# Strassen steps of an MLP behind linear attention on Trainium2: which engine makes the low parts, and when the weight sets are made

## The chip, the cores and the metric

The kernel runs on one core of a Trainium2 chip. [...] An engine works through its queue in order; semaphores make it wait for others. The metric is the time of one execution in microseconds, lower is better.

## What is computed

Linear attention over 8 batches and 8 heads, with a feature map of exponentials, and behind it an MLP on its output, all in float32. Cut to what matters:

```python
def phi(x):
    proj = np.einsum('bhsd,df->bhsf', x, w_phi)
    proj = proj - np.max(np.abs(proj), axis=-1, keepdims=True)
    return np.concatenate([np.exp(proj), np.exp(-proj)], axis=-1)
q_p, k_p = (phi(q), phi(k))
kv = np.einsum('bhsf,bhsd->bhfd', k_p, v)
z = np.sum(k_p, axis=2)
num = np.einsum('bhsf,bhfd->bhsd', q_p, kv)
den = np.einsum('bhsf,bhf->bhs', q_p, z)[..., None] + 1e-06
# x: num / den, as 4608 tokens of 512 features
h = x @ w_in          # 512 x 2048
g = h - np.tanh(h)
return (g @ w_out).astype(np.float32)   # 2048 x 512
```

## The kernel before

**The attention** runs over 32 units of one batch and two heads. `ramp` starts the first three, `period(i)` runs for units 3 to 31 and `drain` ends them. A period takes five units at different stages: it projects unit i, sums the keys of unit i-1 (`kadd`, four operations on POOL), multiplies unit i-2 (`num`), computes the denominator of unit i-3, and divides and stores unit i-5 (`den_mul` on POOL, `x_store` on SP's queue). The denominator goes through DRAM: `den_recip_load` loads it as tile dn, DVE takes the reciprocal (L409), `den_store` writes rr, and in the next period `den_spread` reads it back as rb on all partitions; `den_mul` waits for rb. These DMAs, `x_store` and the loads of v all stand in SP's queue.

In each period DVE also decodes one tile of the weights, which arrive as 64-bit floats: 16 of w_in ("i") and 16 of w_out ("o"), 128x512 each.

**The second stage** multiplies x by w_in with Strassen's seven products instead of eight. Tokens go in 6 groups of 768, features in 8 sets k of two tiles: 48 steps q = 8g + k, called frames. Each product is six matmuls of 384 columns, as both operands are split into a high part in a rounded format and a low part, the remainder (high x high, high x low, low x high). `Prep` makes a set's seven weight operands, high and low: four sums (`sums`, `sums2`), four casts on ACT (`hi`), four subtractions on POOL (`lo`). Sets 0 and 1 are made in the attention (`aside_at`), sets 2 to 7 in frames 0 to 5, two frames ahead. A finished set lies in one of three ring slots; frames 0 to 7 store it to DRAM (`ring_store`, one DMA of 1792 KB), later frames load it two ahead (`ring_load`).

A frame issues, in this order on PE: products p1 and p2, a chunk, p6, a chunk, p5 and p7, a chunk, p4 and p3, a chunk. The products accumulate in two PSUM banks, A and B, that have one buffer each. ACT copies A after p1, p6 and p5 (`part`, L748) and at the end (L762); DVE adds B to these copies: `add11` (L752) after p2, `add22` (L755) after p7, `add21` (L759) after p4. So p4 waits for `add22`, and the next p2 for `add21`. The adds give h as two tiles of 128x768, x (its diagonal quarters) and y (the others). g = h - tanh(h) is then a chain for each: squares, tanh and a mask on ACT (`a_sq`, `a_th`, `a_mk`), five operations on DVE (`v_1`, `v_23` which is two, `v_4`, `v_5`), and the split into a cast on ACT (`a_gh`, L796) and the low part gl on POOL (L797). The chain of y runs in the next frame, between that frame's own adds. A chunk multiplies half of such a tile by w_out, 9 matmuls of 512 columns, six chunks behind its products (`LAG`).

`hooks` places the rest: for group g+1 four operand sums (`x_sum`) and seven operand splits (`x_op`: cast on ACT, low part `x_low`), mostly on POOL, in frames 6 and 7 and the next frame 0; six evictions of finished results (`evict`) in frame 1; in group 0 also `Prep` and `wo_split`, the high and low parts of w_out (the first four are made in the attention). All queues are in the order in which the Python code is written (manual schedule).

Of the kernel before, what the change touches and what calls it, by code (L numbers as in the profile page):

```python
# [33 lines left out]
def tile_linear_attention_moe(  # L34
# [21 lines left out]
    EARLY_O = 4  # L56
    EARLY_K = 2
# [8 lines left out]
    XO_FIRST = (0, 1, 6)  # L66
    assert PC % HT == 0 and NCT == 4 and DM == 4 * P
# [32 lines left out]

    class Prep:
        def __init__(self, k, tags):
            self.k, self.tags = k, tags

        def steps(self):
            w0, w1 = (wi[2 * self.k + n] for n in range(2))
            a, b = slice(0, 2 * P), slice(2 * P, 4 * P)
            sub = nc.gpsimd.tensor_tensor

            def sums():  # L110
                self.r = ring_tile(self.k)
                self.s = [st_any(t, [P, 2 * HT], f"s{self.k}_{t}")[:, 0:DM].rearrange("p (n f) -> p n f", n=2) for t in self.tags]
                s = self.s
                sub(s[0][:, 1], w1[:, a], w1[:, b], ALU.add)
                sub(s[1][:, 0], w0[:, a], w1[:, a], ALU.subtract)

            def sums2():
                s = self.s
                sub(s[0][:, 0], s[0][:, 1], w0[:, a], ALU.subtract)
                sub(s[1][:, 1], w0[:, b], s[0][:, 0], ALU.subtract)  # L120

            def hi(n, m, src):
                nc.scalar.copy(self.r[:, 0, n:m], src())

            def lo(n, m, src):
                sub(self.r[:, 1, n:m], src(), f32(self.r[:, 0, n:m]), ALU.subtract)
# [4 lines left out]
            return [
                (None, sums),
                (None, sums2),
# [973 lines left out]
```

## Time and profile before

| what | us |
|---|---|
| runs before | 1175.53 median of 3 (1172.7 to 1176.58) |
| profiled execution | 1174.16, its span 1172.4 |
| PE busy | 1096.5 (94% of the span) |
| DVE busy | 1005.7 (86%) |
| ACT busy | 847.3 (72%) |
| POOL busy | 636.9 (54%) |

The profile is of one execution. "Busy" adds up the times in which an engine worked, so an average hides stages that have different limits; the prediction therefore reads it by stage. Rows of the timeline give start and duration in us, engine, line, operation, what was written and read, and in brackets the idle time ahead of it with what ended it. Rows of groups give total busy us and the mean in ns. Rows of waits give who waited for whom: us in total, times, longest.

### The profile page before, as it was taken

The page shows a single profiled execution, that of the slowest core. Times are in us where ns is not written, and L with a number is a line of the kernel's source. Part 1 is how long each engine was busy: PE and PEld are TensorE (multiplying, and loading weights), DVE is VectorE, ACT ScalarE, POOL GpSimd, SP SyncE. Part 2 cuts the span into 40 slices and gives each one's busy share as a digit, 9 for nine tenths or more (in the row PEclk, how much of TensorE's full clock was granted, in tenths as well). Part 3 has the DMA queues.
Part 4 walks back from the last instruction along what each step waited for, and adds up shares of the span by engine and source line. Part 5 has one row for each costly group of instructions (what it writes and reads, how often), then busy time and mean ns, then how long its engine had stood idle before and what let it go on. Part 6 is the DMA issues. An engine that isn't in the chain of part 4 may idle for free.

```text
span 1172.4 us, 19032 instructions
## 1 busy us (share of the span) xinstructions
PE 1096.5 (94%) x7244; PEld 909.2 (78%) x7244; DVE 1005.7 (86%) x1062; ACT 847.3 (72%) x1321; POOL 636.9 (54%) x397
## 2 busy tenths in 40 slices
PE   8999999999878788899989999999998999889998
PEld 6666666676567677788878898878987889778986
DVE  7999988999878788988889878988789888898777
ACT  5787887777766566777767776777767777677775
POOL 4788787877598986622464225532356224632222
PEclk9999999999979888999999999999999999999999
DMA  5677778766624124245313541344232443234301
GB/s 179 189 230 218 220 222 250 217 210 192 212 112 180 63 87 165 70 184 200 136 63 145 185 153 66 126 166 148 109 126 73 170 180 126 78 142 149 126 1 55
DMA packets 57676, 173.57 MB, mean 148 GB/s; under 512 B 13680, under 2 KB 28400, under 8 KB 51440
## 3 DMA queue, kind: packets, MB, share of 16 engines
q1 hardware_dynamic: 43184, 139.97, 34.0%
q10 hardware_dynamic: 14400, 32.38, 9.2%
q8 instruction: 57, 0.93, 0.3%
q14 instruction: 35, 0.29, 0.1%
HBM read 138.48 MB, written 33.70 MB: 147 GB/s over the span
## 4 chain that ended last, share of the span: by engine, by line
PE 54%; DVE 27%; ACT 8%; issue 4%; POOL 3%; DMA 2%; POOLq 0%; DVEq 0%; SPq 0%; ACTq 0%
PE A L708 9%; PE B L708 7%; PE pc L322 6%; PE po L819 5%; PE po L820 5%; PE po L825 5%; DVE thy L788 5%; PE po L371 5%; DVE s2y L785 4%; DVE s2y L784 3%; PE pu L385 3%; DVE s2y L791 3%; PE pj L256 2%; DVE s1x L781 2%; PE pa L256 2%
## 5 line engine op out<-in xcount | busy, mean ns | idle before, releaser
L797 POOL TENSOR_TENSOR glx<-s2x,ghx 128x768 fp32r<-128x768 f32 x48 | 103.1, 2149 | 290.8 <-ACT ghx L796 282.7
L708 PE MATMUL A<-xo,wr 128*128 128x384 f32 x1152 | 245.5, 350 | 5.3 <-ACT u L748 4.0
L708 PE MATMUL B<-xo,wr 128*128 128x384 f32 x864 | 185.5, 350 | 53.1 <-DVE hx L755 45.7
L708 PEld LDWEIGHTS A<-xo,wr 128*128 128x128 f32 x1152 | 215.6, 196 | 20.1 <-ACT u L748 5.0
L708 PEld LDWEIGHTS B<-xo,wr 128*128 128x128 f32 x864 | 157.1, 195 | 68.4 <-DVE hx L755 57.9
L797 POOL TENSOR_TENSOR gly<-s2y,ghy 128x768 fp32r<-128x768 f32 x47 | 92.2, 1962 | 133.3 <-ACT ghy L796 119.6
L748 ACT COPY u<-A 128x384 f32<-128x384 f32 x144 | 69.2, 481 | 101.4 <-PE A L708 100.8
L781 DVE SCALAR_TENSOR_TENSOR s1x<-s1x,yx 128x768 f32<-128x768 f32 x48 | 62.4, 1300 | 80.7 <-ACT s1x L770 80.2
L796 ACT CAST ghy<-s2y 128x768 fp32r<-128x768 f32 x47 | 39.2, 835 | 108.2 <-DVE s2y L791 108.2
L819 PE MATMUL po<-who,ghx 128*128 128x512 f32 x288 | 117.4, 407 | 0.0
L820 PE MATMUL po<-wlo,ghx 128*128 128x512 f32 x288 | 116.0, 403 | 0.0
L820 PE MATMUL po<-wlo,ghy 128*128 128x512 f32 x288 | 113.4, 394 | 0.0
L819 PE MATMUL po<-who,ghy 128*128 128x512 f32 x288 | 113.3, 393 | 0.0
L785 DVE SCALAR_TENSOR_TENSOR s2y<-s2y,hy 128x768 f32<-128x768 f32 x48 | 106.5, 2218 | 1.7
L311 ACT ACTIVATE kp<-t 64x256 f32<-64x256 f32 (+1 forms) x126 | 88.4, 726 | 2.1 <-DVE t L275 1.0
L825 PE MATMUL po<-who,glx 128*128 128x512 f32 x288 | 83.0, 396 | 6.9 <-POOL glx L797 6.9
L788 DVE TENSOR_TENSOR thy<-hy,thy 128x768 f32<-128x768 f32 x47 | 74.4, 1583 | 10.1 <-ACT thy L775 10.1
L825 PE MATMUL po<-who,gly 128*128 128x512 f32 x282 | 80.2, 392 | 0.0
L322 PE MATMUL pc<-kp,v 128*64 128x256 f32 x640 | 76.1, 384 | 0.0
L422 POOL TENSOR_TENSOR d<-d,rb 128x576 f32<-128x576 f32 x32 | 46.8, 1462 | 50.3 <-DMA rb<-rr 31.7
L791 DVE COPY_PREDICATED s2y<-yy,thy 128x768 f32<-128x768 uint32 x47 | 67.6, 1439 | 5.6 <-ACT u L748 0.5
L825 PEld LDWEIGHTS po<-who,glx 128*128 128x128 f32 x288 | 53.7, 188 | 21.6 <-POOL glx L797 9.5
(184 smaller groups left out, 2640.3 us busy)
## 6 DMA issues: line engine op xcount, KB each, us to landing
wr<-wd SPq DMA_DIRECT2D x40, 1792.0 KB, 7.3
qk<-in_qkT ACTq DMA_DIRECT2D x27, 576.0 KB, 6.0
wd<-wr SPq DMA_DIRECT2D x8, 1792.0 KB, 5.6
v<-in_v SPq DMA_DIRECT2D x32, 320.0 KB, 4.4
rb<-rr SPq DMA_DIRECT2D x64, 144.0 KB, 4.4
xs<-d SPq DMA_DIRECT2D x32, 288.0 KB, 5.7
out<-o SPq DMA_DIRECT2D x35, 256.0 KB, 2.0
rawo<-in_moe_w_out ACTq DMA_DIRECT2D x16, 512.0 KB, 4.4
```

Of the source, the lines that this page charges most:

```text
L311: nc.scalar.activation(u.kp[h, :, j, s, :], u.t[r][h, :, x, :], AF.Exp, scale=1.0 - 2.0 * s)
L322: nc.tensor.matmul(u.pc[e * D : (e + 1) * D, 0 : 2 * F], u.v[:, j, e, :], u.kp[:, e, j, :, :], start=(j == first), stop=(j == last))
L708: nc.tensor.matmul(bank[:, 0:HT], w[:, a, n, cs], x[:, b, c, :], start=start and i == 0, stop=i == 5, skip_group_check=not start,)
L748: nc.scalar.copy(t, A[q][:, 0:HT])
L781: nc.vector.scalar_tensor_tensor(z.s1, z.s1, PC1, z.y, ALU.add, ALU.mult)
L785: nc.vector.scalar_tensor_tensor(z.s2, z.s2, PA, z.h, ALU.mult, ALU.mult)
L788: nc.vector.tensor_tensor(z.th, z.h, z.th, ALU.subtract)
L791: nc.vector.copy_predicated(z.s2, z.y.bitcast(U32), z.th)
L797: nc.gpsimd.tensor_tensor(z.gl, z.s2, f32(z.gh), ALU.subtract)
L819: nc.tensor.matmul(po, z.gh[:, ts], wh, start=first, stop=False)
L820: nc.tensor.matmul(po, z.gh[:, ts], wl, start=False, stop=False)
L825: nc.tensor.matmul(po, z.gl[:, ts], wh, start=False, stop=last)
```

## The change

1. **POOL's work of the second stage goes to DVE**: gl (`v_gl`), the operand sums and low parts, the low parts of w_out (but three in the head). DVE's order gets `v_gl(xp)` between `v_2` and `v_3`, and `v_gl(yp)` behind `add22`. The high parts of w_out all go to ACT, and five of six evictions too. The operand work of the next group spreads over frames 4 to 7 and the next frame 0.
2. **Seven weight sets are made in the attention** (2 to 6, then 0 and 1), on POOL and ACT, and stored from there in pieces; the order in which weight tiles are decoded follows. Set 7 is made by DVE in frames 2 to 4. Low parts of w_out are no longer made in the attention.
3. **The ring is in pieces**: three tiles a set (products 0 and 1; 2 and 3; 4 to 6), two slots instead of three, each loaded when its products of two frames before are done.
4. **The first two steps are interleaved**: `drain` makes the operands of group 0 and the first two products between the last attention steps, and `head` runs steps 0 and 1 together on two pairs of PSUM banks, with the chain of x of step 0 in two halves.

```diff
-    EARLY_O = 4
-    EARLY_K = 2
+    EARLY_K = 7
+    EARLY_O = 3
+    XS = 10
...
-    wd = [dram.tile([P, 14 * 2 * P], F32, name=f"wd{k}") for k in range(NFP)]
+    PARTS = ((0, 2), (2, 4), (4, 7))
+    wd = [[dram.tile([P, 2 * (b - a) * 2 * P], F32, name=f"wd{k}_{a}") for a, b in PARTS] for k in range(NFP)]
...
+    order = [*range(2, EARLY_K), 0, 1, *range(EARLY_K, NFP)]
+    outs = [("o", f) for f in range(NF)]
+    tiles = []
+    for n, k in enumerate(order):
+        tiles += [("i", 2 * k), ("i", 2 * k + 1), outs[n]]
+    tiles += outs[NFP:]
...
+    def ring_store(q, n, a=0, b=None, queue=nc.sync):
+        queue.dma_start(wd[q % NFP][n][:, a:b], flat(ring[q][n])[:, a:b])
...
+        aside = collections.defaultdict(lambda: ([], [], []))
+        for n, k in enumerate(order[:EARLY_K]):
+            p = Prep(k, nc.gpsimd, early_tile, early_stage).steps()
+            o = 5 + 7 * (n // 2) + 3 * (n % 2)
+            acts = ((1, "h2"), (2, "h4 h6"), (3, "h0")) if n % 2 == 0 else ((2, "h2 h6"), (3, "h4 h0"))
+            work = (
+                ((0, "s1 s3 s2"), (1, "s4 l2"), (2, "l4 l6"), (3, "l0"))
+                if n % 2 == 0
+                else ((0, "s1"), (1, "s3 s2 s4"), (2, "l2 l6"), (3, "l4 l0"))
+            )
+            for which, x in enumerate((acts, work)):
+                for d, names in x:
+                    aside[o + d][which].extend(p[nm] for nm in names.split())
+            if True:
+                when = (3, 4, 5, 5) if n % 2 else (2, 3, 4, 5)
+                for d, (part, a, b) in zip(when, ((1, 0, 1024), (2, 0, 768), (2, 768, 1536), (0, 0, 1024))):
+                    aside[o + d][2].append(lambda k=k, part=part, a=a, b=b: ring_store(k, part, a, b))
+        aside[30][1].extend(lambda n=n: x0_sum(n) for n in range(2))
+        aside[31][1].append(lambda: x0_sum(2))
+
+        def aside_at(i, late):
+            for f in aside[i][0] if not late else aside[i][1] + aside[i][2]:
+                f()
...
-            act, low = aside_at(i)
-            if act:
-                act()
+            if i < NU - 1:
+                aside_at(i, False)
...
             kadd(c)
-            if low:
-                low()
+            aside_at(i, True)
...
+            x0_sum(3, nc.vector)
+            x0_split(1)
...
+            w = dec[NU - 2]
+            dec_0(w, ps_t.tile([P, 2, 512], F32, tag="pt", name="pt"))
+            num_copy(p)
+            dec.append(dec_load(NU - 1, nc.scalar))
             pu = bank()
+            denom(p, pu)
+            dec_1(w)
+            dec_2(w)
+            dec_3(w)
+            ops(2)
+            num(c)
+            lows[2]()
+            den_mul(r)
             ksum(c, pu)
-            denom(p, pu)
...
+            product(A[0], 0, 0, 0, True)
...
+            product(Bk[0], 0, 1, 1, True)
...
-            num(c)
-            w = dec[NU - 1]
-            dec_0(w, ps_t.tile([P, 2, 512], F32, tag="pt", name="pt"))
+            ops(3)
             num_copy(c)
+            ops(6, 5, 4)
             dec_1(w)
             dec_2(w)
             dec_3(w)
+            for m in (3, 6, 5, 4):
+                lows[m]()
             denom(c, bank())
             denom_copy(c)
...
-            nc.scalar.copy(z.gh, z.s2)
-            nc.gpsimd.tensor_tensor(z.gl, z.s2, f32(z.gh), ALU.subtract)
...
+            nc.scalar.copy(z.gh[:, s], z.s2[:, s])
+
+        def v_gl(z, s=ALL):
+            nc.vector.tensor_tensor(z.gl[:, s], z.s2[:, s], f32(z.gh[:, s]), ALU.subtract)
...
-            nc.gpsimd.tensor_tensor(o, a, b, ALU.subtract)
...
+            nc.vector.tensor_tensor(o, a, b, ALU.subtract)
+
+        def ring_load(q, n):
+            nc.sync.dma_start(flat(ring_tile(q, n)), wd[q % NFP][n])
...
+        def head():
+            X0, X1 = slice(0, HT), slice(HT, 2 * HT)
+            ring_load(2, 0)
+            part(0, "u1")
+            add11(0)
+            ps_o.tile([P, 512], F32, tag="o", name="o")
+            p1p2(1, ps_o, "oo")
...
+            p6(0)
+            part(1, "u1")
+            add11(1)
...
+            part(0, "u2")
+            a_th(x, X0)
+            v_1(x, X0)
+            v_2(x, X0)
...
+            p5(0)
+            p7(0)
+            part(1, "u2")
+            part(0, "u4")
+            ring_load(2, 1)
+            a_gh(x, X0)
+            p5(1)
...
+            add22(0)
+            v_gl(x, X0)
+            a_sq(x, X1)
...
+            splits = [wo_split(f, nc.gpsimd if f < EARLY_O else nc.vector) for f in range(4)]
+            for f in (0, 1):
+                for step in splits[f]:
+                    step()
...
+            p4(0)
+            p3(0)
+            ring_load(2, 2)
+            add21(0)
+            a_mk(x, X1)
+            v_3(x, X1)
...
+            p7(1)
+            add22(1)
+            v_gl(x, X1)
+            v_1(y)
+            chunk(6)
+            p4(1)
+            add21(1)
+            v_2(y)
+            p3(1)
...
+            chunk(7)
+            v_5(y)
+            for f in (2, 3):
+                splits[f][0]()
+            a_sq(X[1])
+            a_gh(y)
+            for f in (2, 3):
+                splits[f][1]()
...
+        def late_head():
+            x, y = X[1], Y[0]
+            a_th(x)
+            v_1(x)
+            v_gl(y)
+            a_mk(x)
+            v_2(x)
+            v_3(x)
+            v_4(x)
...
+            if q == 2:
+                late_head()
+            else:
                 a_sq(yp)
-            if xp:
                 v_5(xp)
                 a_gh(xp)
...
+            if q == 2:
+                a_sq(yp)
+                v_5(xp)
+                a_gh(xp)
...
-            if yp:
-                v_1(yp)
-                a_th(yp)
-                v_23(yp)
+            v_1(yp)
+            a_th(yp)
+            v_2(yp)
+            v_gl(xp)
+            v_3(yp)
...
-            if yp:
-                a_gh(yp)
+            if q == 2:
+                v_4(yp)
+                v_5(yp)
+            a_gh(yp)
             at("a6")
+            v_gl(yp)
...
-            p4p3(q)
+            p4(q)
+            p3(q)
...
+            if q + 2 < NQ:
+                for n, at in enumerate(("a2", "a5", "end")):
+                    h[at].append(lambda n=n: ring_load(q + 2, n))
+            if g and k == 0:
+                op("a4", g, 6, "a6")
+            if g and k == 1:
+                for t, at in enumerate(("a2", "a2", "a3", "a5", "a5", "a6")):
+                    h[at].append(lambda t=t: evict(g - 1, t, nc.vector if t == 1 else nc.scalar))
+            if nxt < NG:
+                if k == (2 if g else 4):
+                    h["end" if g else "a2"].append(lambda: x_loads(nxt))
+                if 4 <= k < 7:
+                    for n in ((0, 1), (2,), (3,))[k - 4]:
+                        h["a3" if g else "end"].append(lambda n=n: x_sum(nxt, n))
+                    op("a4" if g else "end", nxt, k - 4, "a6" if g else "end")
+                if k == 7:
+                    op("a2", nxt, 3, "a3")
+                    op("a4", nxt, 4, "a6")
+                    op("end", nxt, 5, "end")
             if g == 0:
-                h["start"].append(lambda: ring_store(q))
...
-                op("a2", g, 4, nc.gpsimd, "a2")
-                op("a4", g, 5, nc.gpsimd, "a4")
-                op("a5", g, 6, nc.vector, "a6")
-            if g and k == 1:
-                h["a2"].append(lambda: evict(g - 1, 0, nc.scalar))
-                h["a2"].append(lambda: evict(g - 1, 1, nc.vector))
-                h["a3"].append(lambda: evict(g - 1, 2, nc.scalar))
-                h["a5"].append(lambda: evict(g - 1, 4, nc.scalar))
-                h["a6"].append(lambda: evict(g - 1, 3, nc.vector))
-                h["a6"].append(lambda: evict(g - 1, 5, nc.vector))
...
-                if k == 6:
-                    for n, at in enumerate(("start", "a2", "a4")):
-                        h[at].append(lambda n=n: x_sum(nxt, n))
-                    op("a4", nxt, 0, nc.gpsimd, "a6")
-                if k == 7:
-                    op("a2", nxt, 1, nc.gpsimd, "a2")
-                    op("a4", nxt, 2, nc.gpsimd, "a4")
-                    op("a5", nxt, 3, nc.vector, "a6")
-                    h["a4"].append(lambda: x_sum(nxt, 3))
-            if g == 0:
-                if k + 2 < NFP:
-                    steps = Prep(k + 2, (3, 4)).steps()
-                    for (act, pool), at in zip(steps, ("start", "start", "a2", "a4", "a6", "end")):
-                        if act:
-                            h[at].append(act)
-                        h[at].append(pool)
-                for n, at in ((0, "a6"), (1, "end")):
-                    f = EARLY_O + 2 * k + n
...
+                for p in PREP.values():
+                    for kk, at, names in (
+(2, "end", "s1 s3 s2 s4"),
+                        (3, "a3", "h2 l2 h4"),
+                        (3, "end", "l4 h6"),
+                        (4, "a3", "l6"),
+                        (4, "end", "h0 l0"),
...
+                for n, at in enumerate(("a6", "a7")):
+                    f = 2 * k + n
+
+                    def hi(f=f):
+                        split[f] = wo_split(f, nc.vector)
+                        split[f][0]()
+
+                    h["a1"].append(hi)
+                    h[at].append(lambda f=f: split[f][1]())
...
-        for q in range(NQ):
+        head()
+        for q in range(2, NQ):
             frame(q)
```

Three places in the queues. First DVE in frame 43, from the operation behind y's `v_2` to x's `v_5`; the names are those of the chain above (hx and hy are h, u the copies of A). Before:

```order
L785 SCALAR_TENSOR_TENSOR s2y_10300<-s2y_10300,hy_10262 128x768
L788 TENSOR_TENSOR thy_10329<-hy_10262,thy_10329 128x768
L791 COPY_PREDICATED s2y_10300<-yy_10298,thy_10329 128x768
L755 TENSOR_TENSOR hx_10309<-B_10281,u_43_10351 128x384
L781 SCALAR_TENSOR_TENSOR s1x_10374<-s1x_10374,yx_10373 128x768
L759 TENSOR_TENSOR hy_10392<-B_10281,u_43_10326 128x384
L784 SCALAR_TENSOR_TENSOR s2x_10375<-s2x_10375,s1x_10374 128x768
L785 SCALAR_TENSOR_TENSOR s2x_10375<-s2x_10375,hx_10309 128x768
L788 TENSOR_TENSOR thx_10394<-hx_10309,thx_10394 128x768
L791 COPY_PREDICATED s2x_10375<-yx_10373,thx_10394 128x768
```

and now:

```order
L907 TENSOR_TENSOR glx_10555<-s2x_10494,ghx_10554 128x768
L892 SCALAR_TENSOR_TENSOR s2y_10549<-s2y_10549,hy_10511 128x768
L895 TENSOR_TENSOR thy_10579<-hy_10511,thy_10579 128x768
L898 COPY_PREDICATED s2y_10549<-yy_10547,thy_10579 128x768
L856 TENSOR_TENSOR hx_10557<-B_10531,u_43_10602 128x384
L907 TENSOR_TENSOR gly_10614<-s2y_10549,ghy_10613 128x768
L886 SCALAR_TENSOR_TENSOR s1x_10627<-s1x_10627,yx_10626 128x768
L860 TENSOR_TENSOR hy_10645<-B_10531,u_43_10574 128x384
L889 SCALAR_TENSOR_TENSOR s2x_10628<-s2x_10628,s1x_10627 128x768
L892 SCALAR_TENSOR_TENSOR s2x_10628<-s2x_10628,hx_10557 128x768
L895 TENSOR_TENSOR thx_10647<-hx_10557,thx_10647 128x768
L898 COPY_PREDICATED s2x_10628<-yx_10626,thx_10647 128x768
```

The two low parts, L907, stand where none stood: one ahead of y's third operation and so ahead of the second add (L856), one right behind that add, ahead of x's first operation and the third add (L860).

POOL in a period in the middle of the attention (d is the result that `den_mul` scales, ss the key sum, wr a weight set). Before:

```order
L422 TENSOR_TENSOR d_1532<-d_1532,rb_1722 128x576
L332 TENSOR_TENSOR ss_1824<-kp_131 128x512
L333 TENSOR_TENSOR ss_1824<-ss_1824,kp_131 128x512
L334 TENSOR_TENSOR ss_1824<-ss_1824,kp_131 128x512
L335 TENSOR_TENSOR ss_1824<-ss_1824,kp_131 128x512
L126 TENSOR_TENSOR wr_1438<-s_4_1440,wr_1438 128x512
```

and now:

```order
L492 TENSOR_TENSOR d_1567<-d_1567,rb_1765 128x576
L402 TENSOR_TENSOR ss_1869<-kp_147 128x512
L403 TENSOR_TENSOR ss_1869<-ss_1869,kp_147 128x512
L404 TENSOR_TENSOR ss_1869<-ss_1869,kp_147 128x512
L405 TENSOR_TENSOR ss_1869<-ss_1869,kp_147 128x512
L168 TENSOR_TENSOR wr_2_1836<-s_4_1606,wr_2_1836 128x512
L168 TENSOR_TENSOR wr_2_1836<-wi_1423,wr_2_1836 128x256
```

In such a period before, one operation of a set stood behind the key sum, and only in six periods for each of two sets; now one to three stand there in periods 5 to 29.

SP's queue in a period of the attention (xs is the result's store). Before:

```order
L425 DMA xs_86<-d_1532 128x576
L404 DMA dn_1849<-dd_1847 128x1x9
L419 DMA rb_1851<-rr_1777 64x576 x2
L236 DMA v_1854<-in_v 128x640
L414 DMA rr_1906<-rn_1904 128x9
```

and now:

```order
L495 DMA xs_86<-d_1567 128x576
L112 DMA wd_2_102<-wr_1_1703 128x1024
L474 DMA dn_1896<-dd_1894 128x1x9
L489 DMA rb_1898<-rr_1820 64x576 x2
L306 DMA v_1901<-in_v 128x640
L484 DMA rr_1953<-rn_1951 128x9
```

A store of a piece of a weight set (wd) stands between the result's store and the load of the denominator dn, ahead of rb and v.

More of the change, by code (lines that the diff above doesn't have):

```diff
@@ new lines, in x_op, with product @@
+    def x_op(g, m, eng):
+        if m in xop.get(g, {}):
+            x = xop[g][m]
+            src = f32(x[:, 1])
+        else:
+            x, src = x_tile(g, m), xst[g, XSRC[m]]
+        nc.scalar.copy(x[:, 0], src)
+        return lambda: x_low(eng, x, src)
+    def product(bank, q, n, m, start):
+        x = xop[q // NFP][m]
+        part = [i for i, (a, b) in enumerate(PARTS) if a <= n < b][0]
+        w = ring[q][part]
+        n -= PARTS[part][0]
+        i = 0
+        for c in range(2):
+            cs = slice(c * P, (c + 1) * P)
+            for a, b in ((0, 0), (0, 1), (1, 0)):
+                nc.tensor.matmul(
+                    bank[:, 0:HT],
+                    w[:, a, n, cs],
+                    x[:, b, c, :],
+                    start=start and i == 0,
+                    stop=i == 5,
+                    skip_group_check=not start,
+                )
+                i += 1
@@ L107, in steps @@
             a, b = slice(0, 2 * P), slice(2 * P, 4 * P)
[L108 to L126, printed above, removed]
+            def sub(o, x, y, op=ALU.subtract):
+                self.eng.tensor_tensor(o, x, y, op)
             def two(w):
                 return w.rearrange("p (n f) -> p n f", f=2 * P)
[L131 to L138 removed]
+            def s1():
+                self.s = [two(t) for t in self.stage(self.k)]
+                sub(self.s[0][:, 1], w(1)[:, a], w(1)[:, b], ALU.add)
@@ new lines, in tile, with hi, lo, f @@
+            def tile(n, m):
+                i = [x for x, (a, b) in enumerate(PARTS) if a <= n < b][0]
+                if i not in self.r:
+                    self.r[i] = self.ring_tile(self.k, i)
+                c = PARTS[i][0]
+                return self.r[i][:, 0, n - c : m - c], self.r[i][:, 1, n - c : m - c]
+            def hi(n, m, src):
+                return lambda: nc.scalar.copy(tile(n, m)[0], src())
+            def lo(n, m, src):
+                def f():
+                    h, l = tile(n, m)
+                    sub(l, src(), f32(h))
+                return f
@@ L936, in frame @@
             a_mk(X[q])
-            v_23(X[q])
+            v_2(X[q])
+            v_3(X[q])
             v_4(X[q])
@@ L1020, in finish @@
             chunk(s + 1)
-            v_23(yp)
+            v_2(yp)
+            v_gl(xp)
+            v_3(yp)
             a_mk(yp)
```

295 lines of the change are left out of this document (153 added, 142 removed).

## The prediction

> **What bounds the kernel now.** I first read the busy time by stage, because one average hides three different limits. Columns: length, busy us of each engine with its instruction count, granted TensorE clock, DMA share, GB/s.
>
> ```profile
> 0.00:314.00 314.00, 307.70 (x3500) 213.23 (x3500) 277.20 (x383) 241.19 (x466) 233.27 (x194) 1.00 0.70 210
> 314.00:455.00 141.00, 111.29 (x480) 95.68 (x472) 116.26 (x102) 88.52 (x132) 120.49 (x75) 0.87 0.33 131
> 455.00:1172.00 717.00, 677.53 (x3273) 600.29 (x3273) 612.24 (x578) 517.61 (x724) 283.16 (x128) 0.98 0.34 124
> ```
>
> The attention (0 to 314) is TensorE's: PE is busy 98% of it. In the next stretch POOL is the fullest (85%) and PE falls to 79%. Behind it PE has 94% and DVE 85%. To see how long one step of the second stage (a frame) takes, I followed its one add of the first quarter in the timeline:
>
> ```profile
> 321.66 0.55 DVE L752 TENSOR_TENSOR hx<-B,u 128x384 f32<-128x384 f32 x1
> ...
> 356.25 0.54 DVE L752 TENSOR_TENSOR hx<-B,u 128x384 f32<-128x384 f32 x1
> ...
> 483.97 0.55 DVE L752 TENSOR_TENSOR hx<-B,u 128x384 f32<-128x384 f32 x1
> ...
> 757.41 0.54 DVE L752 TENSOR_TENSOR hx<-B,u 128x384 f32<-128x384 f32 x1
> ...
> 893.52 0.54 DVE L752 TENSOR_TENSOR hx<-B,u 128x384 f32<-128x384 f32 x1
> ...
> 1125.72 0.56 DVE L752 TENSOR_TENSOR hx<-B,u 128x384 f32<-128x384 f32 x1
> 1141.42 0.56 DVE L752 TENSOR_TENSOR hx<-B,u 128x384 f32<-128x384 f32 x1
> ```
>
> These are frames 0, 2, 8, 24, 32, 46 and 47. The last two lie 15.70 us apart, and around them PE has no gap:
>
> ```profile
> 1094.00:1141.00 47.00, 47.00 (x236) 42.29 (x235) 37.62 (x40) 34.49 (x49) 11.85 (x6) 1.00 0.16 59
> ```
>
> So 15.7 us is PE's own floor for a frame. Frames 2 to 8 take 127.7 us for six (21.3 each), and a whole group of eight (24 to 32) 136.1 (17.0 each), where eight floors are 125.6. Who costs the difference stands in the waits from 455 on:
>
> ```profile
> POOL glx L797 <- ACT ghx L796: 282.7, 41, 7.9
> ...
> DVE s1x L781 <- ACT s1x L770: 70.7, 38, 2.2
> PEld B L708 <- DVE hx L755: 42.0, 20, 5.3
> ```
>
> PE waits for DVE's second add (L755), in 20 frames of 42. DVE is late because of POOL:
>
> ```profile
> 945.27 2.09 POOL L797 TENSOR_TENSOR glx<-s2x,ghx 128x768 fp32r<-128x768 f32 x1 [7.39 <-ACT ghx L796]
> 945.67 2.50 DVE L785 SCALAR_TENSOR_TENSOR s2y<-s2y,hy 128x768 f32<-128x768 f32 x1
> L785 DVE SCALAR_TENSOR_TENSOR s2y<-s2y,hy x42: 957/2499/2556, 467.1 to 1159.1; 128x768 f32<-128x768 f32 x42
> ```
>
> In the last row the three durations are lowest, median and highest: 957 ns alone, 2499 beside POOL. The DVE operation ends 0.81 us after POOL's, its whole own time, so it waited for POOL's to end.
>
> **The sum's terms: later groups.** POOL's operations of the groups go to DVE; what DVE's cost undisturbed:
>
> ```profile
> L781 DVE SCALAR_TENSOR_TENSOR s1y<-s1y,yy x42: 936/958/961, 465.1 to 1157.1; 128x768 f32<-128x768 f32 x42
> L784 DVE SCALAR_TENSOR_TENSOR s2x<-s2x,s1x x42: 940/942/2144, 458.4 to 1153.2; 128x768 f32<-128x768 f32 x42
> L788 DVE TENSOR_TENSOR thx<-hx,thx x42: 946/951/953, 461.4 to 1155.1; 128x768 f32<-128x768 f32 x42
> L791 DVE COPY_PREDICATED s2x<-yx,thx x42: 1071/1085/1100, 462.4 to 1156.1; 128x768 f32<-128x768 uint32 x42
> L850 DVE TENSOR_TENSOR xo<-xst1b,xo x1: 949/949/949, 494.4 to 494.4; 128x768 fp32r<-128x768 f32 x1
> L1030 DVE TENSOR_TENSOR gly<-s2y,ghy x2: 558/558/559, 1163.4 to 1165.7; 128x384 fp32r<-128x384 f32 x2
> L834 DVE COPY o<-po 128x512 f32<-128x512 f32 x17 | 11.2, 682 | 1.7 <-issue 1.4 <-PE po L825 0.4
> ```
>
> A low part gl on DVE is the same work as L850: 0.95 us. A frame on DVE is then 3 adds (0.54) + 2 x (0.96 + 0.94 + 0.96 + 0.95 + 1.09 + 0.95) = 13.3 us. A group adds four operand sums and seven operand low parts (11 x 0.95) and one eviction (0.68): 8 x 13.3 + 10.5 + 0.7 = 117.6, under PE's 125.6. But DVE also waits: between v_5(y) and v_1(x) ACT has to cast and make two squares, while DVE has the add and gl (1.5 us).
>
> ```profile
> L796 ACT CAST ghx<-s2x 128x768 fp32r<-128x768 f32 x42 | 34.5, 821 | 2.2 <-DVE s2x L791 2.2
> L769 ACT ACTIVATE yx<-hx 128x768 f32<-128x768 f32 x41 | 34.5, 841 | 0.0
> L770 ACT ACTIVATE s1x<-yx,bias_t 128x768 f32<-128x768 f32 x41 | 38.5, 939 | 1.3
> L832 ACT COPY o<-po 128x512 f32<-128x512 f32 x18 | 10.5, 591 | 0.9 <-PE po L822 0.9
> ```
>
> 0.82 + 0.84 + 0.94 = 2.6, less 1.5: 1.1 us a frame, 8.8 a group, together 126.4. DVE and PE thus tie, and I take one us more for the frame in which ACT makes five evictions instead of three (2 x 0.59): 127.4 a group, 15.9 a frame. Frames 8 to 47 are 39 intervals: now 1141.4 - 484.0 = 657.4; then 39 x 15.9 = 620. **Term: -37.** With no friction at all it would be 39 x 15.7 = 612 (-45). Behind v_gl in DVE's queue stand v_3 and the second add, for which PE waits; PE needs that add one chunk after the product that frees it: a chunk is 4608 of a frame's 34560 columns, 2.1 us of 15.7. Less the add's 0.54 that leaves about 1.5 to spare, and the two operand sums (1.9) of one frame in eight eat it.
>
> [...]
>
> **First group.** POOL's six remaining sets and twelve low parts of w_out leave this stretch. DVE keeps, for frames 2 to 8: 6 x 13.3; twelve low parts of w_out (0.69 each, between the 0.56 for 384 and 0.95 for 768 columns); ten operand sums and low parts (9.5); and one weight set (four sums of 256 columns at 0.42, as the copy of that size below, and low parts of 512, 512, 512 and 256: 4.2). That is 79.8 + 8.3 + 9.5 + 4.2 = 101.8, and 2 for waits: 104. DVE is the bound here, not PE (6 x 15.7 = 94). Now 127.7: -24.
>
> The head runs from the last unit's copy to frame 2's first add:
>
> ```profile
> 310.47 0.41 DVE L364 COPY kv<-pc 128x256 f32<-128x256 f32 x1
> 311.99 0.70 DVE L213 TENSOR_SCALAR pt<-pt 128x512 uint32<-128x512 uint32 x1
> ```
>
> That is 45.8 us now (to 356.25). Of steps 0 and 1 PE has 14 products (2304 columns, 1.05 us each) and two chunks, about 19 us, so DVE's queue sets it: two decodes (8 x 0.70), five operand low parts (4.75), seven adds (3.8), two half-width chains (12 x 0.56), the whole chain of y0 (5.8), four operations of x1 (3.8), one low part (0.7): 31 us. POOL's three low parts beside it (1.28 each) lock DVE out for up to 3.9; I take 2, and 2 for ACT: 35. -11. **Term: -35.**
>
> **The attention.** Seven sets instead of two are made beside it, and 28 stores that lay behind it come in. POOL's prices, a cast on ACT and its wait, and three stretches: without loads of x, with four of them, and one period alone:
>
> ```profile
> L335 POOL TENSOR_TENSOR ss<-ss,kp 128x512 f32<-128x512 f32 x21 | 27.0, 1284 | 1.7
> L422 POOL TENSOR_TENSOR d<-d,rb 128x576 f32<-128x576 f32 x22 | 31.1, 1416 | 37.0 <-DMA rb<-rr 20.5 <-PE pj L256 5.4 <-DMA v<-in_v 4.7
> L126 POOL TENSOR_TENSOR wr<-wi,wr 128x256 fp32r<-128x256 f32 x1 | 0.7, 747 | 0.0
> L154 ACT CAST who<-wo 128x512 fp32r<-128x512 f32 x4 | 2.4, 608 | 0.0
> ACT dd L399 <- PE pu L343: 47.4, 28, 1.9
> ...
> 109.01:165.68 56.67, 56.67 (x656) 39.33 (x654) 51.81 (x74) 46.16 (x90) 46.27 (x37) 1.00 0.73 218
> 165.68:224.16 58.48, 57.35 (x656) 39.65 (x654) 51.70 (x73) 45.60 (x88) 46.35 (x35) 1.00 0.82 239
> 224.16:233.58 9.42, 9.42 (x111) 6.56 (x109) 8.62 (x14) 7.29 (x15) 8.60 (x8) 1.00 0.74 220
> ...
> wd<-wr SPq DMA_DIRECT2D x8, 1792.0 KB, 5.6
> ```
>
> A period costs POOL 4 x 1.28 + 1.42 = 6.6. A set is four sums and one low part of 256 columns (0.75) and three low parts of 512 (1.28), 7.6 us; over 3.5 periods 2.2 each, in the worst one 2.6. 8.8 to 9.2 fit into 9.42, and the single period shows 8.60 with no delay. The casts (two of 0.61 in a period) stand where ACT waits 47.4 / 28 = 1.7 us for the denominator. So POOL and ACT hide it; if their cover goes, the whole excess of a period shows. The DMAs do not hide: the stretch with four extra loads of 384 KB took 58.48 against 56.67 for six periods, 1.8 us more, about 0.5 for each, because SP's queue brings dn and rb later and DVE waits for dn. Now 28 stores of 384 or 512 KB stand directly ahead of dn, in pieces of 3 or 4 KB a partition where those loads' have 1.5. The ends are 0 (all hidden) and 7 x 5.6 = 39 (each store's whole time is added); by the nearest row, 28 x 0.5 = 14. I take 13. **Term: +13.**
>
> **The sum.** The profiled execution took 1174.16 us, 1.76 beyond its span, and lies 1.4 under the median 1175.53. 1174.2 - 37 - 35 + 13 = **1115 us**; the tail behind frame 47 (31 us) stays.
>
> **Rivals.** *DVE's queue binds every frame* (13%): the waits for ACT, which POOL's idle 282.7 us took in silence, now stand in DVE's order, and groups stay at 17.0 a frame. 1174 - 35 + 13 = 1152. For it: DVE and PE tie. Against it: the 1.1 us fits.
> *Each store pays in full* (11%): 1174 - 37 - 35 + 39 = 1141. Each would hold dn and rb for its 1.2 to 1.6 us behind it in SP's queue. [...]
> *All is hidden* (10%): the attention stays, and all frames from 2 on run at 15.7: 1174 - 45 - 33 - 11 = 1085.
> *Slower* (4%): POOL becomes the attention's bound, since its wait for rb comes on top of a full program.
>
> ```profile
> POOL d L422 <- DMA rb<-rr: 27.4, 16, 3.0
> ```
>
> With its longest wait every period is 9.2 + 3.0 = 12.2, +2.8 in 25 periods, 70 us, and the stores 39: 1174 - 72 + 109 = 1211. It decides from 2.9 us a period. Against it: the mean wait is 1.7, mostly slack of an engine with little to do.
> *The change doesn't leave POOL idle* (2%): the order shows only two multiplications there behind the head, and then the time would stay near 1174.
>
> **Chances.** My forecast has 60%, with 1100 to 1130 of its own. The range goes from 1088, where nearly all is hidden, to 1150, which takes in the full stores and most of the DVE rival. Faster by over 0.3% (about what a measurement can tell from no change): 95%; within it 1%; slower 4%.
>
> **What would show it.** Frames 40 to 47 at 15.7 to 16.0 with PE full: right on the groups. L907 near 0.95 us and no DVE operation at 2.5: the price is right. Frames 2 to 8 near 104 us, with PE waiting for DVE: right on the first group. The attention's end near 327 with waits of L479 for dn: right on the stores; at 314 I was too dark, at 350 the full price holds. I would be wrong if DVE waits for ACT more than 2.4 us in each frame, or POOL for rb in each period.

## The result: 1099.1 us, and the profile after

| | us |
|---|---|
| changed kernel | 1099.09 median of 4 runs (1098.22 to 1100.9) |
| kernel before | 1175.44 median of 4 (1172.7 to 1176.58) |
| ratio | 0.9356, 95% interval 0.9335 to 0.9376 |
| profiled span | 1096.4 (before 1172.4) |

The time lies in the range (1088 to 1150), 16 us under the forecast of 1115. In the rows PE is TensorE, with its matmuls, DVE is VectorE, ACT ScalarE and POOL GpSimd, and SP's queue holds the DMAs named here. The windows by stage come first again: length, busy us of PE, weight load, DVE, ACT and POOL with their instruction counts, granted clock, DMA share, GB/s.

```profile
0.00:325.00 325.00, 311.02 (x3484) 213.04 (x3485) 278.19 (x385) 248.75 (x481) 263.87 (x229) 1.00 0.78 241
325.00:457.00 132.00, 122.85 (x611) 107.68 (x611) 124.17 (x160) 109.48 (x168) 6.28 (x4) 0.99 0.45 147
457.00:1096.00 639.00, 634.47 (x3152) 569.77 (x3150) 557.90 (x665) 502.68 (x702) 3.10 (x2) 1.00 0.41 136
```

POOL is idle behind the attention, and PE is busy 99% of the last stretch (94% before). The timeline rows of the frames' first adds, here L853, of frames 2, 8, 24, 32, 46 and 47:

```profile
359.39 0.55 DVE L853 TENSOR_TENSOR hx<-B,u 128x384 f32<-128x384 f32 x1
...
456.73 0.54 DVE L853 TENSOR_TENSOR hx<-B,u 128x384 f32<-128x384 f32 x1
...
707.39 0.56 DVE L853 TENSOR_TENSOR hx<-B,u 128x384 f32<-128x384 f32 x1
...
832.53 0.55 DVE L853 TENSOR_TENSOR hx<-B,u 128x384 f32<-128x384 f32 x1
...
1051.22 0.56 DVE L853 TENSOR_TENSOR hx<-B,u 128x384 f32<-128x384 f32 x1 [0.60 <-PE B L142]
1066.87 0.56 DVE L853 TENSOR_TENSOR hx<-B,u 128x384 f32<-128x384 f32 x1 [0.60 <-PE B L142]
```

A group (24 to 32) takes 125.1 us, 15.64 a frame. The last frame takes 15.65, and in it DVE waits for PE: every frame of the later groups runs at PE's floor. The waits from 457 on say the same from the other side. DVE waits for ACT 0.7 us in each frame, and PE hardly ever waits for the second add any more (42.0 us in the weight load's row before):

```profile
DVE s1x L886 <- ACT s1x L874: 26.8, 40, 1.2
...
PEld B L142 <- DVE hx L856: 2.8, 4, 1.4
```

The groups of instructions (line, operation, count; busy us, mean ns; idle time ahead with what ended it) give the price of the moved work. The low parts cost 0.95 and 0.96 us on DVE, and no group of s2y stands at 2.5 any more:

```profile
L907 DVE TENSOR_TENSOR glx<-s2x,ghx 128x768 fp32r<-128x768 f32 x41 | 39.0, 951 | 0.0
L892 DVE SCALAR_TENSOR_TENSOR s2y<-s2y,hy 128x768 f32<-128x768 f32 x41 | 39.0, 951 | 0.0
L907 DVE TENSOR_TENSOR gly<-s2y,ghy 128x768 fp32r<-128x768 f32 x40 | 38.5, 962 | 3.3 <-ACT ghy L904 2.9
```

The attention became longer. The copies of the key-value products of units 30 and 31 stand at 314.04 and 320.90, where 301.81 and 310.47 stood before, and one wait has grown: between 30 us and the attention's end DVE waits 21.2 us for dn, where it waited 2.9 in the kernel before (from 30 to 305 us). POOL's wait for rb has not grown (24.9 against 27.4). Here are the changed kernel's two copies, then DVE's wait for dn in the kernel before, then the two waits in the changed one:

```profile
314.04 0.41 DVE L434 COPY kv<-pc 128x256 f32<-128x256 f32 x1
...
320.90 0.42 DVE L434 COPY kv<-pc 128x256 f32<-128x256 f32 x1
```

```profile
DVE rn L409 <- DMA dn<-dd: 2.9, 4, 1.1
```

```profile
POOL d L492 <- DMA rb<-rr: 24.9, 18, 3.3
DVE rn L479 <- DMA dn<-dd: 21.2, 15, 3.0
```

By the prediction's own terms, each measured between the same two instructions in both traces:

| term | forecast | measured |
|---|---|---|
| attention, to the last unit's copy | +13 | +10.4 (+12.2 to the copy of unit 30) |
| head, from there to frame 2 | -11 (to 35) | -7.3 (45.8 to 38.5) |
| frames 2 to 8 | -24 (to 104) | -30.4 (127.7 to 97.3) |
| frames 8 to 47 | -37 (to 620) | -47.3 (657.4 to 610.1) |
| tail | 0 | -1.4 |
| sum | -59 | -76.0, the whole difference of the spans |

### The profile page after: what moved, and what is told of

The parts are those of the page before. It is cut to its first block, busy times and chain, and to the rows that moved or that the text cites. A ratio compares the mean times of both kernels' runs of the same rounds, so it can differ in the third digit from the quotient of the medians.

```text
span 1096.4 us, 19205 instructions
## 1 busy us (share of the span) xinstructions
PE 1068.3 (97%) x7244; PEld 890.5 (81%) x7244; DVE 960.3 (88%) x1208; ACT 860.9 (79%) x1349; POOL 273.2 (25%) x235
## 4 chain that ended last, share of the span: by engine, by line
PE 76%; DVE 9%; DMA 7%; ACT 3%; issue 2%; SPq 1%; POOL 1%; DVEq 0%; ACTq 0%; POOLq 0%
PE A L142 16%; PE B L142 12%; PE po L930 11%; PE po L929 11%; PE po L935 10%; PE pc L392 4%; DMA dn<-dd 4%; PE po L441 3%; DMA rb<-rr 3%; PE pj L326 2%; PE pu L455 2%; PE pa L326 2%; PE ptt L356 2%; DVE t L345 1%; DVE m L344 1%
## 5 line engine op out<-in xcount | busy, mean ns | idle before, releaser
L142 PE MATMUL A<-xo,wr 128*128 128x384 f32 x1152 | 234.6, 339 | 4.9 <-ACT u L849 2.8
L142 PEld LDWEIGHTS A<-xo,wr 128*128 128x128 f32 x1152 | 206.0, 188 | 19.2 <-ACT u L849 3.9
L142 PE MATMUL B<-xo,wr 128*128 128x384 f32 x864 | 176.6, 339 | 3.2 <-DVE hx L856 3.2
L929 PE MATMUL po<-who,ghx 128*128 128x512 f32 x288 | 113.0, 392 | 0.5 <-DVE hy L860 0.5
L886 DVE SCALAR_TENSOR_TENSOR s1x<-s1x,yx 128x768 f32<-128x768 f32 (+1 forms) x49 | 46.2, 942 | 29.0 <-ACT s1x L874 28.5
L441 PE MATMUL po<-qe,kv 128*64 128x288 f32 x512 | 68.0, 408 | 1.6 <-ACT d L465 1.6
L935 PEld LDWEIGHTS po<-who,gly 128*128 128x128 f32 x282 | 52.9, 188 | 11.9 <-DVE gly L907 0.2
L392 PEld LDWEIGHTS pc<-kp,v 128*64 128x64 f32 x640 | 43.0, 136 | 23.8 <-issue 4.7
L929 PEld LDWEIGHTS po<-who,ghy 128*128 128x128 f32 x288 | 54.0, 188 | 10.3 <-ACT ghy L904 2.0
L929 PEld LDWEIGHTS po<-who,ghx 128*128 128x128 f32 x288 | 54.0, 188 | 9.2 <-DVE hy L860 0.9
```

The lines of the kernel that those rows point to most:

```text
L142: nc.tensor.matmul(bank[:, 0:HT], w[:, a, n, cs], x[:, b, c, :], start=start and i == 0, stop=i == 5, skip_group_check=not start,)
L392: nc.tensor.matmul(u.pc[e * D : (e + 1) * D, 0 : 2 * F], u.v[:, j, e, :], u.kp[:, e, j, :, :], start=(j == first), stop=(j == last))
L441: nc.tensor.matmul(u.po[e * D : (e + 1) * D, c, 0:CH], u.kv[:, s, e * D : (e + 1) * D], u.qe[:, e, s, c * CH : (c + 1) * CH], start=(s == ...
L886: nc.vector.scalar_tensor_tensor(z.s1[:, s], z.s1[:, s], PC1, z.y[:, s], ALU.add, ALU.mult)
L929: nc.tensor.matmul(po, z.gh[:, ts], wh, start=first, stop=False)
L935: nc.tensor.matmul(po, z.gl[:, ts], wh, start=False, stop=last)
```

## The experiments

Each diff is against the changed kernel. The time is that of the run; "frames 8 to 47" is measured between the first adds.

**1. The stores behind dn.** The 28 stores of weight sets go to the place behind dn, rb and v in SP's queue, in the same periods. Bytes, and POOL's work, stay.

```diff
         def aside_at(i, late):
-            for f in aside[i][0] if not late else aside[i][1] + aside[i][2]:
+            for f in aside[i][1] if late else aside[i][0]:
                 f()
...
                 load_v(a)
+            for f in aside[i][2]:
+                f()
             ksum_copy(p)
```

> The changed kernel with one thing moved: in each attention period the stores of weight pieces are issued behind the loads of dn, rb and v in SP's queue instead of ahead of them; same bytes, same work on POOL. Theory (the stores delay dn and rb because they stand ahead of them in SP's queue): DVE's wait for dn falls from 21 us to under 8, the copy of unit 30 on DVE (314.0 us in the changed kernel, 301.8 before) comes at 303 to 308, and the time falls from 1099 to 1088 to 1093. Rival (POOL's fuller program stretches the periods): the copy stays at 313 to 315 and the time at 1099. Second rival (the DMA engines are simply too full, wherever the stores stand): the wait moves to rb or xs and the copy stays above 310.

1089.61 us, median of 4 runs (1086.71 to 1090.31), ratio to the kernel before 0.9278 (0.9262 to 0.9293). The same two copies, and the same two waits of this kernel:

```profile
302.75 0.42 DVE L434 COPY kv<-pc 128x256 f32<-128x256 f32 x1
...
309.62 0.42 DVE L434 COPY kv<-pc 128x256 f32<-128x256 f32 x1
```

```profile
POOL d L492 <- DMA rb<-rr: 18.4, 13, 4.2
...
DVE rn L479 <- DMA dn<-dd: 3.0, 6, 1.0
```

In this trace the attention is back within 0.9 us of before (301.81), with seven sets made in it: of its 12.2 us, 11.3 belonged to the place of the stores in the queue. The trace is that of the shortest of the four runs; the medians of the two kernels lie 9.5 us apart. Experiment 8 has the stores in the same place, and its trace, of the longest of its runs, has the copy at 305.70. So a store costs 0.4 us ahead of dn and 0.03 to 0.14 behind it. POOL still waits 18.4 us for rb, and the attention is as short as before all the same. This version beats both kernels.

**2. Few stores.** Sets 2 to 6 and 0 aren't stored (24 of 28 stores left out), and where they would be loaded set 1 is loaded instead, so this kernel computes something else in the same number of steps.

```diff
-            if True:
+            if n == EARLY_K - 1:
                 when = (3, 4, 5, 5) if n % 2 else (2, 3, 4, 5)
...
-            nc.sync.dma_start(flat(ring_tile(q, n)), wd[q % NFP][n])
+            nc.sync.dma_start(flat(ring_tile(q, n)), wd[q % NFP if q % NFP >= EARLY_K else 1][n])
```

> The changed kernel with 24 of the 28 stores of weight pieces in the attention left out; only set 1 is stored, and steps 2 and later load set 1 in place of the sets that were not stored (as many loads as before; the result is not the reference's). POOL and ACT make all seven sets as in the changed kernel. Theory (the stores cost the attention its 12 us): the copy of unit 30 at 302 to 305 instead of 314.0, wait for dn under 5 us. Rival (POOL's five further sets cost it): it stays at 312 to 315. Frames 2 to 47 should not change by more than 2 us.

1085.43 us in one run; the copy of unit 30 at 301.10, DVE's wait for dn 3.0 us, frames 8 to 47 in 610.33. Without nearly all the stores the attention is 1.7 us shorter than in experiment 1, with all of them behind dn, and 4.6 us shorter than in experiment 8. So POOL's 24 us of added work (229.8 us between 30 and 290, against 205.5 in almost the same stretch before) are no part of the 12 us, and what the bytes of the stores cost by themselves is at most these few us.

**3. gl back on POOL.** Only the low parts of g return there; the rest of the change stays.

```diff
         def v_gl(z, s=ALL):
-            nc.vector.tensor_tensor(z.gl[:, s], z.s2[:, s], f32(z.gh[:, s]), ALU.subtract)
+            nc.gpsimd.tensor_tensor(z.gl[:, s], z.s2[:, s], f32(z.gh[:, s]), ALU.subtract)
```

> The changed kernel with all low parts gl back on POOL, at the same places in the order; operand sums and operand low parts stay on DVE. Rival to test, as my prediction told it (gl on POOL locks DVE out and makes it late, so gl is what the groups gained by): frames 8 to 47 go from 610 back towards 657, at least 640. Theory after seeing both traces (in a frame without operand work gl cost DVE about 1.6 us of lock, 0.957 to 2.5 for one operation, about as much as the 1.9 us it costs DVE to do both itself; what cost the groups was the operand work on POOL): frames 8 to 47 take 612 to 628.

**4. The operands back on POOL.** Only the operand sums and operand low parts return.

```diff
         def x_sum(g, n):
...
-            nc.vector.tensor_tensor(o, a, b, ALU.subtract)
+            nc.gpsimd.tensor_tensor(o, a, b, ALU.subtract)
...
-                h[at].append(lambda: keep.append(x_op(g, m, nc.vector)))
+                h[at].append(lambda: keep.append(x_op(g, m, nc.gpsimd)))
```

> The changed kernel with the operand sums and operand low parts of groups 1 to 5 back on POOL, at the same places in the order; gl stays on DVE. Theory (operand work on POOL, 2.5 us an operation, locks DVE out and comes late for PE): frames 8 to 47 take 635 to 657 instead of 610, with DVE operations beside them at 2 to 2.6 us. Rival (gl was what counted): frames 8 to 47 stay below 620.

**5. Both back on POOL:** the edits of 3 and 4 together.

> The changed kernel with gl and the operand sums and low parts of the groups all back on POOL, at the new places in the order (operand work spread over five frames). If the two costs (12 us for gl, 19 for the operand work on POOL, each tried alone) add up: frames 8 to 47 take 638 to 645, and the rest of the 657 before came from where the operand work and the evictions stood. If spreading gained nothing: 652 to 662.

1123.83, 1123.69 and 1175.87 us, one run each. Frames 8 to 47 took 622.4, 629.0 and 673.7 (610.1 in the changed kernel). The rest of the longer times is mostly in frames 2 to 8, where the same work moved (104.8, 105.6 and 111.2, against 97.3), and in the attention, which varies by itself (last section). Here are the windows over just these frames: the changed kernel, then gl, operands, and both on POOL.

```profile
456.73:1066.87 610.14, 609.06 (x3035) 548.30 (x3034) 536.81 (x638) 484.34 (x676) 3.10 (x2) 1.00 0.42 140
```

```profile
468.81:1091.20 622.39, 614.59 (x3031) 545.42 (x3030) 532.19 (x561) 480.54 (x676) 166.16 (x80) 1.00 0.41 137
```

```profile
463.48:1092.47 628.99, 611.92 (x3034) 547.00 (x3034) 555.62 (x594) 485.06 (x676) 113.05 (x47) 1.00 0.40 136
```

```profile
469.43:1143.16 673.73, 630.74 (x3038) 559.59 (x3037) 555.73 (x516) 481.07 (x677) 269.71 (x125) 0.98 0.37 127
```

Read the third pair of figures, DVE. With gl on POOL DVE has 77 instructions less and is busy only 4.6 us less; with the operands there, 44 less and 18.8 us more; with both, 122 less and 18.9 us more. What POOL takes from DVE's queue it gives back as lock, which is what I call the time that a DVE operation waits for a POOL operation to end. Two rows of the first of these kernels show one case, POOL's and DVE's timeline:

```profile
935.25 2.55 POOL L907 TENSOR_TENSOR glx<-s2x,ghx 128x768 fp32r<-128x768 f32 x1 [6.74 <-ACT ghx L904]
```

```profile
936.12 2.50 DVE L892 SCALAR_TENSOR_TENSOR s2y<-s2y,hy 128x768 f32<-128x768 f32 x1
938.53 0.95 DVE L967 TENSOR_TENSOR xst5t<-xst5b,xst5t 128x768 f32<-128x768 f32 x1
```

s2y starts 0.87 us behind glx and ends 0.82 behind its end. The next operation, which has no POOL beside it, takes 0.95. The operands cost more than gl though POOL makes only 47 operations instead of 80.

gl alone landed where the theory put it; the operands alone came out between the theory and its rival. Together they came out above both ranges (638 to 645 and 652 to 662). The two returns do not add: 12.3 and 18.8 alone, 63.6 together. That a spare which each of them used alone is then used up (experiments 6 and 7 measure it) fits this, but is argued, not shown.

Whether PE waits for POOL's results themselves, and not for DVE, can be read from PE's waits in frames 8 to 47. The first two rows are of the kernel before, the third is of the kernel with both on POOL:

```profile
PE B L708 <- DVE hx L755: 25.7, 13, 3.5
PE B L708 <- POOL xo L850: 6.8, 5, 1.5
```

```profile
PE B L142 <- DVE hx L856: 41.9, 22, 2.9
```

Before, PE also waited once a group for a low part of an operand made by POOL, which the prediction didn't mention. At the new places in the order no wait of PE for POOL is left in any of these three kernels: nearly all that PE waits for is the second add, in DVE's queue, and with both on POOL that wait is longer than before.

The kernel with both takes as long as the one before (1175.9 against 1175.5), although its seven sets, its ring and its interleaved head are those of the changed kernel. It saves in frames 2 to 8 (127.7 to 111.2) and loses as much in the later frames (657.4 to 673.7). Why these are longer than before isn't shown; POOL makes all the operand low parts there, while in the kernel before DVE made 9 of the 31 in frames 8 to 47, so this kernel doesn't price the spreading alone. So the rest of the change gains nothing without part 1. Part 1 without the rest was not tried.

**6. One more operation in each frame on DVE:** from group 1 on the low part of y is made twice.

```diff
             v_gl(yp)
+            if g:
+                v_gl(yp)
             chunk(s + 2)
```

> The changed kernel with one DVE operation more in each frame of groups 1 to 5: the low part of y is made twice, 0.95 us each (same result). My prediction's account (117.6 us of work and 8.8 of waits tie a group on DVE with PE's 125.6): 0.95 x 8 = 7.6 us more a group must show, frames 8 to 47 take 640 to 650 instead of 610. Theory after the traces (the waits for ACT are slack that a later DVE uses up, so DVE has some 7 us free in a group): frames 8 to 47 take 611 to 622.

**7. Two more:** that of x, ahead of the second add, as well.

```diff
             v_gl(xp)
+            if g:
+                v_gl(xp)
             v_3(yp)
...
             v_gl(yp)
+            if g:
+                v_gl(yp)
             chunk(s + 2)
```

> The changed kernel with two DVE operations more in each frame of groups 1 to 5: the low parts of x and y are both made twice (same result). DVE then has 117.6 + 15.2 = 132.8 us of work in a group of 125.2: with no wait left at all frames 8 to 47 take 39 x 16.6 = 647, and more with waits. If they stay below 640, DVE's count by rows is wrong.

1096.5 and 1125.96 us, one run each. The first costs nothing: frames 8 to 47 take 610.33 us, against 610.14 in the changed kernel. Windows over frames 8 to 47, one more and two more:

```profile
454.75:1065.08 610.33, 609.10 (x3035) 548.32 (x3034) 569.99 (x677) 483.49 (x676) 3.91 (x2) 1.00 0.42 140
```

```profile
459.94:1093.90 633.96, 617.96 (x3036) 548.04 (x3035) 604.84 (x717) 481.32 (x677) 3.42 (x2) 1.00 0.40 135
```

DVE's idle time fell from 73.3 us (610.14 - 536.81) to 40.3 at no cost. With the second it stays at 29.1, and the frames grow by 23.6, 0.6 us each. The waits of these two kernels, from 475 on, show what was used up. One more:

```profile
DVE s1x L886 <- ACT s1x L874: 1.3, 5, 0.3
```

Two more:

```profile
PEld B L142 <- DVE hx L856: 26.0, 26, 2.6
PE B L142 <- DVE hx L856: 14.9, 25, 2.1
...
DVE s1x L886 <- ACT s1x L874: 1.2, 5, 0.2
```

The 26.8 us for which DVE waited for ACT have all but gone: they are no cost that comes on top, they are the space into which DVE's next work goes. With two more PE waits for the second add again. The expectation of at least 647 was too high although it held no wait at all. It had said itself that below 640 DVE's count by rows is wrong, and it is: 132.8 us a group were expected, and DVE was busy 604.8 us in these frames, 124 a group.

**8. The stores behind dn, and the head without POOL:** experiment 1 with the first three low parts of w_out on DVE.

```diff
-            splits = [wo_split(f, nc.gpsimd if f < EARLY_O else nc.vector) for f in range(4)]
+            splits = [wo_split(f, nc.vector) for f in range(4)]
```

> The changed kernel with the stores behind dn, rb and v, as before, and the three low parts of w_out in the head moved from POOL to DVE (3 x 0.69 us). If POOL's operations lock DVE out in the head (three half-width operations took 1.0 us more each there): from the last unit's copy on DVE to frame 2's first add 35 to 37 us instead of 37.3, and the time 1086 to 1090, about as without it. If the lock cost nothing: 38.5 to 39.5, 2 us slower.

1090.21 us, median of 4 (1086.2 to 1090.87), not told apart from experiment 1 (1089.61). The windows of the head, from the last unit's copy to frame 2's first add, with POOL (experiment 1) and without:

```profile
309.62:346.93 37.31, 30.44 (x174) 24.75 (x175) 32.67 (x45) 29.46 (x53) 8.80 (x6) 1.00 0.46 152
```

```profile
312.57:351.30 38.73, 31.59 (x173) 25.44 (x174) 31.09 (x48) 29.39 (x53) 3.92 (x3) 0.96 0.46 146
```

DVE makes three operations more and is busy 1.6 us less, so the lock was there. The head is not shorter for it: 38.7 lies in the range given for a lock that costs nothing, and DVE has 7.6 us idle now where it had 4.6. Most of the difference is a new wait: the moved low parts stand in DVE's queue until ACT has made their cast.

```profile
333.66 1.29 DVE L224 TENSOR_TENSOR wlo<-wo,who 128x512 fp32r<-128x512 f32 x2 [2.17 <-ACT who L223]
```

## Why the prediction held, and where its sizes were off

**Later groups (-37, measured -47.3).** Direction and mechanism hold: experiments 3 to 5 bring the time back by undoing this part alone, and PE then waits for the second add again. The mis-sized term is "117.6 + 8.8 + 1 a group". Two things in it were wrong. First, the 117.6 added up durations, and DVE's recorded durations overlap. Timeline of the changed kernel, DVE:

```profile
355.79 0.95 DVE L907 TENSOR_TENSOR gly<-s2y,ghy 128x768 fp32r<-128x768 f32 x1
356.66 0.95 DVE L889 SCALAR_TENSOR_TENSOR s2x<-s2x,s1x 128x768 f32<-128x768 f32 x1
357.64 0.96 DVE L892 SCALAR_TENSOR_TENSOR s2x<-s2x,hx 128x768 f32<-128x768 f32 x1
358.52 0.95 DVE L895 TENSOR_TENSOR thx<-hx,thx 128x768 f32<-128x768 f32 x1
359.39 0.55 DVE L853 TENSOR_TENSOR hx<-B,u 128x384 f32<-128x384 f32 x1
```

The operation at 355.79 takes 0.95, and the next, which does not read its result, starts 0.87 later; the one at 357.64 reads the s2x of the one at 356.66 and starts 0.98 later. Over frames 8 to 47 of this trace the distance behind an operation of 0.93 to 0.97 was 0.86 to 0.88 in 241 of the 245 cases in which the next did not read its result, and 0.98 to 1.07 in all 150 in which it did. The durations between frames 8 and 47 add up to 568.5 (forecast: 573), while DVE was busy 536.8, 110 a group instead of 117.6. Second, the waits for ACT do not come on top. They were there as forecast (26.8 + 11.0 for s1y + 2.9 for gly, 8.1 a group, by the waits from 457 on), but experiment 6 uses them up without cost. DVE and PE therefore do not tie: PE has the frame, and DVE has about 1.1 us of spare in each. That is one operation at 0.87, and 0.26 of the second, whose other 0.61 showed.

**Frames 2 to 8 (-24, measured -30.4).** The count was right: the durations there add up to 103.1, the forecast 101.8. The window from frame 2's first add to frame 8's shows what they take:

```profile
359.39:456.73 97.34, 93.58 (x462) 82.50 (x461) 94.76 (x122) 81.86 (x118) 0.00 (x0) 1.00 0.44 147
```

94.8 busy and 2.6 idle (forecast 2): DVE's queue is full, as said, and the error of 6.7 comes from the overlap of durations, 8.3 us.

**Head (-11, measured -7.3).** Here the forecast was too bold. DVE was busy 32.8 us of 38.5, where the forecast had 33 of 35 (31 and 2 of lock). The term that was too small is DVE's waiting: 5.7 us idle, not 2. The lock cost about 3, not 2: two operations of 0.56 took 1.53 and 1.65 beside POOL's low parts, and one of 1.08 took 1.95. Here are POOL's and DVE's timelines of the changed kernel at the first two:

```profile
341.97 2.86 POOL L224 TENSOR_TENSOR wlo<-wo,who 128x512 fp32r<-128x512 f32 x2 [12.68 <-ACT who L223]
```

```profile
342.14 1.53 DVE L892 SCALAR_TENSOR_TENSOR s2x<-s2x,hx 128x384 f32<-128x384 f32 x1
343.59 1.65 DVE L895 TENSOR_TENSOR thx<-hx,thx 128x384 f32<-128x384 f32 x1
```

Experiment 8 shows that taking this lock away as it does gains nothing: the head stays at 37 to 39 (PE's granted clock was 0.96 there and 1.00 in experiment 1, and 1.1 of the 1.4 us between them are PE's busy time). That the chain between ACT, PE and DVE bounds the head is argued from DVE's idle time, not shown. A shorter order of it was not tried, nor were the interleaving and the ring in pieces undone one at a time; their shares stay open.

**Attention (+13, measured +12.2 to unit 30).** Cause and place hold, and experiments 1 and 2 show them. The forecast has no lock of DVE beside POOL's added work in it, and none showed: DVE was busy 236.8 us in experiment 1 (from 30 to 291.7) and 237.0 before (from 30 to 290.8). That the size fits to 1 us is in part luck: with the same code for the attention, six kernels took 9.8 to 17.1 us more than before (last section). The last period came 1.8 us shorter than before, which the forecast did not have.

**The rivals.** *DVE's queue binds every frame* fails, with PE busy 99.8% of frames 8 to 47 and 15.64 us a frame. *Each store pays in full* fails in size: 0.44 us a store (12.2 / 28; 0.35 to 0.61 over the six kernels), not 1.4. The order in the queue that it stood on is real, since moving the same stores behind dn gives 11.3 of the 12.2 us back. *All is hidden* (1085) is right on the frames and wrong on the attention; experiment 1 is about that kernel, at 1089.6. *POOL becomes the attention's bound* fails: experiment 1 keeps POOL's work and loses the cost. (The 2.9 us a period that would decide it leave the stores out; with their 39 us in the sum it would be 1.3.) *POOL not idle* fails by the window row: two instructions behind 457.

## What to carry to other kernels

Count an engine's queue by the distance from one start to the next (0.87 us here), not by adding durations (0.95), and do not add its waits to its work: find how much it can take by putting a useless operation into each step until the time moves (here the first cost 0.2 us in 39 frames, the second 23.6). Undo the parts of a move singly and together: here two parts put back on POOL cost 12.3 and 18.8 us alone, and 63.6 together. In one queue, a store issued ahead of a small load that someone waits for cost the path 0.4 us here; the same store behind it cost 0.03 to 0.14.

## What the runs showed of the hardware that was not expected

**The second add, which reads PSUM, took its usual time beside POOL.** With both on POOL, timeline of POOL and of DVE:

```profile
962.50 2.43 POOL L967 TENSOR_TENSOR xst5b<-xst5b,xst5b 128x768 f32<-128x768 f32 x1
964.89 2.57 POOL L120 TENSOR_TENSOR xo<-xo 128x768 fp32r<-128x768 f32 x1
967.42 1.85 POOL L907 TENSOR_TENSOR gly<-s2y,ghy 128x768 fp32r<-128x768 f32 x1
```

```profile
963.34 2.46 DVE L898 COPY_PREDICATED s2y<-yy,thy 128x768 f32<-128x768 uint32 x1
965.70 0.54 DVE L856 TENSOR_TENSOR hx<-B,u 128x384 f32<-128x384 f32 x1
968.42 1.67 DVE L886 SCALAR_TENSOR_TENSOR s1x<-s1x,yx 128x768 f32<-128x768 f32 x1 [2.19 <-ACT s1x L874]
```

The masked copy, all of it in SBUF, takes 2.46 instead of 1.08 and ends 0.87 behind the end of POOL's operation at 962.50. The second add, which reads B from PSUM, starts while POOL works and takes its usual 0.54; all 40 second adds of frames 8 to 47 in that run took 0.53 to 0.57. That PSUM makes the difference was not tried apart from the rest of the operation. POOL's times differ too: in this run its operand operations of 128x768 take 1.91 to 2.58 us, most of them over 2.5, while gl of y, of the same size, takes 1.83 to 1.87, and the one shown starts while DVE stands idle for 2.19. That DVE delays POOL in turn fits this, but is not shown.

**The granted clock was lower in the stretches where PE waited most.** In frames 2 to 8 it was 0.91 before and 1.00 after, in the head 0.81 and 0.96, and with both on POOL 0.98 in frames 8 to 47. PE was busy 106.9 us in frames 2 to 8 before and 93.6 after. The same shows, weaker, in frames 8 to 47: here is the window of the kernel before, where PE was busy 624.2 us at a clock of 0.99, against 609.1 at 1.00.

```profile
483.97:1141.42 657.45, 624.23 (x3035) 554.61 (x3034) 565.03 (x534) 477.79 (x668) 260.17 (x118) 0.99 0.35 127
```

The forecast had no term for it. How much of the gain is the clock's isn't told apart: with gl on POOL, and with two more operations, PE was busy 614.6 and 618.0 us in these frames at a clock of 1.00. PE's share alone doesn't account for the clock either: PE was busy 82% of the head in experiments 1 and 8, with 1.00 in one and 0.96 in the other.

**The attention varies between kernels whose code for it is the same.** With the stores ahead of dn the copy of unit 30 stood at 314.0, 318.9, 312.5, 313.4, 316.7 and 311.6 us (the changed kernel, gl, operands, one more, two more, both); with them behind dn at 302.75 and 305.70. The two groups stay apart, but a difference of a few us inside one of them says nothing of the edit. Why they vary was not tried.
